# Turning the attention blocks of five batches on VectorE and through HBM instead of on TensorE, in a fused attention and feed-forward kernel

## The chip, the cores and the metric

The program runs on one core of a Trainium2 chip. The metric is the device time of one execution in microseconds (us). Engines are named as in the profile: PE is TensorE (matmuls; PEld its weight loads), DVE is VectorE, ACT is ScalarE, POOL is GpSimd, and SP is the engine that only issues DMAs (SPq its queue). SBUF is the on-chip memory, PSUM the accumulator memory that PE writes, in eight banks; HBM is the memory off the core. Each engine works through its own list of instructions strictly in order.

## The reference

Eight batches of eight heads, 576 positions of 64 channels. The output of attention is the sum of a coarse and a local part; it then goes through a two-layer network with a squared ReLU:

```python
q_d, k_d, v_d = (t.reshape(B, H, S // 4, 4, D).mean(axis=3) for t in (q, k, v))
out_up = np.repeat(sm_attn(q_d, k_d, v_d), 4, axis=2)        # coarse: 144 x 144 per head
scores = np.where(abs(i - j) < 4, scale * q @ k.T, -1e9)      # local: 7 offsets per position
x = (out_up + softmax(scores) @ v).transpose(0, 2, 1, 3).reshape(4608, 512)
y = (s * np.maximum(x @ w_in, 0) ** 2 + b) @ w_out            # 512 -> 2048 -> 512
```

All is fp32. The kernel splits the operands of the two large products into a high and a low part and makes three products of them.

## The kernel before

**The network.** The 4608 tokens are cut into 18 tiles `t` of 256, the 2048 hidden channels into 8 parts `p`. `products1(t, p)` (called G; L631) makes 24 matmuls of 256 columns into a PSUM bank `ph`, for which `split_x` must have made `xh` and `xl` of tile `t` (ACT L612, DVE L613). `upper` (called R; ACT L646 to L648: ReLU, square, cast to `gh`) and `lower` (V; DVE L653: `gl`) follow. `products2(t, p)` (H; L712 to L714) makes 12 matmuls of 512 columns into two banks `po`, in four steps of three (two row halves m, two channel halves j). After part 7 of a tile, `evict_half` (DVE L686) empties each `po` bank into `os`, and a DMA stores it; tile t+1 uses the same two banks. `ph` alternates between two banks, so that G of one (t, p) needs V of the one two before.

**The order of PE's work.** The list `order` holds the 144 pairs (t, p). The first 28 and their surroundings are laid out by a hand-written plan (`PLAN`), which this change leaves alone. From pair 28 (`BEGIN`) on a loop takes two pairs at a time and chains the matmuls by manual dependencies: 3 matmuls of G, one step of H, the rest of the first pair's G, R and V, one step of H, the second pair's G, R and V, six steps of H. At its end eight steps of H are over.

**The attention of batches 3 to 7** (the change's subject) runs beside this. Its unit of work is a *group*: four heads of one batch, in two units of two heads (`down_unit`), ten groups in all.
- *Local part* (`local_unit`), twice per group (halves `h`): `lqk` is loaded into one buffer (768 KB, L530), seven times POOL multiplies (L537, `pr`) and DVE sums (L539, `st`), a softmax of eight small DVE instructions and one ACT exp (L542 to L550), then DVE multiplies by the values (L555, L558, `pv`) and POOL or DVE adds (L559, `acc`). Positions lie on partitions here. Nine PE transposes of 128x128 (L569, `ot`) turn `acc` into the layout of `x` (channels on partitions), and six DVE additions (L573) add it to `x`.
- *Coarse part* (`down`), once per unit: DVE sums q and k by fours (L323, L325), ACT writes q into a block-diagonal operand (L330), PE makes the scores `sa` (L342), DVE and ACT the softmax `pd` (L344 to L357), six PE transposes (L365, L368, L370: `tp`, `tr`) turn it, ACT copies them to SBUF (L373, L376), PE multiplies by the values (L381, L383: `up`), and ACT spreads `up` over `x` (L519). POOL prepares the value operands (L308 to L313) into a place that the unit before's `up` must have read.

`advance` steps this work forward between the pieces of G and H, at a rate given by `need` and `free` (by which pair a batch must be ready, and from which its buffer is free); the framework then orders each engine's list by priority and a schedule of its own.

## Time and profile before

| what | us |
|---|---|
| median of 3 runs (961.5 to 962.66) | 962.63 |
| the profiled execution: its time, its span from first to last instruction | 959.7, 957.9 |
| busy in the span: PE, DVE, ACT, POOL | 924.6, 645.2, 478.2, 412.9 |
| last softmax of the attention (ACT L546) | 740.7 |
| last addition to `x` (DVE L573) | 758.1 |

The span falls into three stages: to about 250 us the plan (loading, the attention of batches 0 to 2, the first G and H); to 758 us the loop of G and H with the attention of batches 3 to 7 beside it; then G and H alone. The change touches the middle stage. In the profile's groups the engine comes behind the line (`L569 PE`), then the operation, then the tile written and the tiles read. An engine's idle time is given with what ended it.

### The profile page before, as it was taken

The page shows a single profiled execution, that of the slowest core. Times are in us where ns is not written, and L with a number is a line of the kernel's source. Part 1 is how long each engine was busy: PE and PEld are TensorE (multiplying, and loading weights), DVE is VectorE, ACT ScalarE, POOL GpSimd, SP SyncE. Part 2 cuts the span into 40 slices and gives each one's busy share as a digit, 9 for nine tenths or more (in the row PEclk, how much of TensorE's full clock was granted, in tenths as well). Part 3 has the DMA queues.
Part 4 walks back from the last instruction along what each step waited for, and adds up shares of the span by engine and source line. Part 5 has one row for each costly group of instructions (what it writes and reads, how often), then busy time and mean ns, then how long its engine had stood idle before and what let it go on. Part 6 is the DMA issues. An engine that isn't in the chain of part 4 may idle for free.

```text
span 957.9 us, 18429 instructions
## 1 busy us (share of the span) xinstructions
PE 924.6 (97%) x7316; PEld 831.1 (87%) x7316; DVE 645.2 (67%) x1134; ACT 478.2 (50%) x1133; POOL 412.9 (43%) x440
## 2 busy tenths in 40 slices
PE   6699999999999999999999999999999999999998
PEld 5588888888889989898999899889898999999997
DVE  9999999844688879787878797787877421211121
ACT  7977775466553636354544454544434333332332
POOL 6401130010587776767676768676776200000000
PEclk9699999999999999999999999999999999999999
DMA  9755413223232323323232323232311000000000
GB/s 327 264 169 179 144 47 114 71 71 102 90 107 96 110 89 108 97 91 111 83 106 81 123 79 126 80 113 91 114 54 43 1 23 1 23 1 23 1 23 22
DMA packets 32022, 86.25 MB, mean 90 GB/s; under 512 B 3520, under 2 KB 8128, under 8 KB 31936
## 3 DMA queue, kind: packets, MB, share of 16 engines
q1 hardware_dynamic: 31936, 85.08, 27.2%
q8 instruction: 57, 0.93, 0.4%
q14 instruction: 29, 0.24, 0.1%
HBM read 75.63 MB, written 9.44 MB: 89 GB/s over the span
## 4 chain that ended last, share of the span: by engine, by line
PE 54%; DVE 18%; POOL 17%; issue 5%; ACT 3%; DMA 2%; DVEq 0%; POOLq 0%; ACTq 0%
PE ph L631 24%; PE po L712 8%; POOL pr L537 8%; PE po L713 8%; PE po L714 8%; POOL acc L559 6%; DVE pv L558 3%; DVE acc L559 2%; DVE gl L653 1%; DVE st L539 1%; DVE bias L669 1%; PE sa L342 1%; DMA lqk<-in_qkn_dram 1%; PE ol L479 1%; DVE es L272 1%
## 5 line engine op out<-in xcount | busy, mean ns | idle before, releaser
L631 PE MATMUL ph<-xh,wi 128*128 128x256 f32 x2176 | 414.0, 280 | 1.6 <-DVE gl L653 1.6
L631 PEld LDWEIGHTS ph<-xh,wi 128*128 128x128 f32 x2176 | 345.2, 189 | 10.7 <-DVE gl L653 2.7
L631 PE MATMUL ph<-xl,wi 128*128 128x256 f32 x1152 | 321.6, 279 | 0.0
L537 POOL TENSOR_TENSOR pr<-lqk 128x576 f32<-128x576 f32 x140 | 206.4, 1495 | 77.0 <-DMA lqk<-in_qkn_dram 53.7
L631 PEld LDWEIGHTS ph<-xl,wi 128*128 128x128 f32 x1152 | 217.4, 189 | 7.3 <-DVE xl L771 0.2
L646 ACT ACTIVATE ph<-ph 128x512 f32<-128x512 f32 x144 | 83.9, 582 | 235.1 <-PE ph L631 227.1
L712 PE MATMUL po<-wo,gh 128*128 128x512 f32 x416 | 166.3, 400 | 4.6 <-DVE os L686 4.5
L713 PE MATMUL po<-wo,gh 128*128 128x512 f32 x416 | 164.0, 394 | 0.0
L714 PE MATMUL po<-wo,gl 128*128 128x512 f32 x416 | 162.8, 391 | 0.8 <-DVE gl L653 0.7
L653 DVE TENSOR_TENSOR gl<-ph,gh 128x512 fp32r<-128x512 f32 x104 | 71.0, 683 | 105.4 <-ACT gh L648 105.0
L539 DVE TENSOR_REDUCE st<-pr 128x9 f32<-128x576 f32 x140 | 106.2, 759 | 48.4 <-POOL pr L537 45.9
L559 POOL TENSOR_TENSOR acc<-acc,pv 128x576 f32<-128x576 f32 x80 | 115.0, 1437 | 54.0 <-DVE pv L558 31.5
L558 DVE TENSOR_TENSOR pv<-lv,st 128x576 f32<-128x576 f32 x120 | 87.3, 745 | 32.4 <-POOL acc L559 32.1
L312 POOL TENSOR_TENSOR dq<-vt 80x64 f32<-80x64 f32 x58 | 20.7, 368 | 174.5 <-PE up L383 173.3
L714 PEld LDWEIGHTS po<-wo,gl 128*128 128x128 f32 x416 | 78.1, 188 | 18.9 <-DVE gl L653 2.1
L712 PEld LDWEIGHTS po<-wo,gh 128*128 128x128 f32 x416 | 78.1, 188 | 18.6 <-DVE os L686 4.4
L713 PEld LDWEIGHTS po<-wo,gh 128*128 128x128 f32 x416 | 78.3, 188 | 11.1 <-issue 0.2
L647 ACT ACTIVATE ph<-ph 128x512 f32<-128x512 f32 x144 | 83.8, 582 | 3.7
L712 PE MATMUL po<-wo,gb 128*128 128x512 f32 x160 | 63.3, 396 | 3.5 <-DVE os L686 3.5
L648 ACT CAST gh<-ph 128x512 fp32r<-128x512 f32 x104 | 61.0, 587 | 9.5 <-PE po L713 6.7
L653 DVE TENSOR_TENSOR gb<-ph,gb 128x512 fp32r<-128x512 f32 x40 | 27.3, 682 | 53.9 <-ACT gb L648 53.9
L713 PE MATMUL po<-wo,gb 128*128 128x512 f32 x160 | 62.9, 393 | 0.0
(158 smaller groups left out, 1243.2 us busy)
## 6 DMA issues: line engine op xcount, KB each, us to landing
tqk<-in_qk_dram SPq DMA_DIRECT2D x30, 584.0 KB, 3.7
lqk<-in_qkn_dram SPq DMA_DIRECT2D x20, 768.0 KB, 4.6
lv<-in_vn_dram SPq DMA_DIRECT2D x20, 480.0 KB, 3.3
out_dram<-os SPq DMA_DIRECT2D x34, 256.0 KB, 2.3
wst<-in_moe_w_in_dram SPq DMA_DIRECT2D x7, 1024.0 KB, 5.9
wst<-in_moe_w_out_dram SPq DMA_DIRECT2D x7, 1024.0 KB, 4.9
tvd<-in_vdm_dram SPq DMA_DIRECT2D x29, 160.0 KB, 2.4
tvr<-in_vr_dram SPq DMA_DIRECT2D x29, 128.0 KB, 2.2
```

Of the source, the lines that this page charges most:

```text
L537: nc.gpsimd.tensor_tensor(pr, lqk[:, 0:CH], lqk[:, CH + o : 2 * CH + o], ALU.mult)
L539: nc.vector.tensor_reduce(ls[:, :, o], pr, AX.X, ALU.add)
L558: nc.vector.tensor_tensor(pv, lv[:, o : o + CH], w, ALU.mult)
L559: (nc.vector if o % 3 == 1 else nc.gpsimd).tensor_tensor(acc[:, :, h], acc[:, :, h], pv, ALU.add)
L631: nc.tensor.matmul(ph[:, j], wi[p][:, s, k, f], xk[:, k], start=k == 0 and s == 0 and xk is xh, stop=k == NK - 1 and s == 1)
L646: nc.scalar.activation(ph, ph, AF.Relu)
L647: nc.scalar.activation(ph, ph, AF.Square)
L648: nc.scalar.copy(gh, ph)
L653: nc.vector.tensor_tensor(gl, acc.pop((t, p)), gh.bitcast(F32), ALU.subtract)
L712: nc.tensor.matmul(po[m], gh[:, j, ms], wo[p][:, 0, j], start=first, stop=False)
L713: nc.tensor.matmul(po[m], gh[:, j, ms], wo[p][:, 1, j], start=False, stop=False)
L714: nc.tensor.matmul(po[m], gl[:, j, ms], wo[p][:, 0, j], start=False, stop=last)
```

## The change

The transposes of batches 3 to 7 leave PE. DVE turns 32x32 blocks (`nc.vector.transpose`) into a tile `ft`; a DMA writes `ft` to a tile in HBM (`far_off`, `away`), and further DMAs read it back with the blocks rearranged, so that store and loads together complete the turn.
- Local part, per group: two DVE transposes of 128x576 for nine PE transposes, one store of 576 KB, four loads of 144 KB, and two DVE additions of 128x576 (from SBUF) for six from PSUM. The additions are put off to the next group's first half, behind its softmax (`late`).
- Coarse part, per unit: two DVE transposes (96x288, 96x192) for six PE transposes and three ACT copies, two stores (108 and 72 KB), seven loads (rows of 384 or 192 bytes) back into the unit's own `pd`; ACT's write of q takes another pattern. `up` is now issued with the next unit's `sa`.
- H lags G by one step more (one step is left out in the loop's second pass; nine are over at the end). `need` of batches 3 to 7 is two pairs earlier. The qk operand is zeroed once more by POOL, and tiles change places.

The core of the diff (in `far_rest` the softmax, in `begin_far` the sums are those of `down`):

```diff
+    far_off = ctx.enter_context(
+        tc.tile_pool(name="far_off", bufs=2, space=bass.MemoryType.DRAM))
...
-    def down_unit(b, hp, banks):
+    @contextlib.contextmanager
+    def behind(engine, before=None):
...
+                tc.add_manual_dep(
+                    i, before.name,
...
+    def begin_far(b, hp):
...
+        for h in range(2):
+            hs = slice(64 * h, 64 * h + 64)
+            nc.scalar.copy(
+                qc[hs].rearrange("p i (r c) -> p i r c", c=32)[:, :, :, 16 * h : 16 * h + 16],
+                qd[hs].rearrange("p (r i c) -> p i r c", r=3, i=NQ))
+        return kd
+
+    def end_far(b, hp, both, banks):
...
+        pm = both[0:KM, 0 : 6 * GQ].rearrange("p (r n) -> p r n", r=3)
+        pr = both[:, 6 * GQ :].rearrange("p (r n) -> p r n", r=3)
+        up = banks([P, SD], "up")
+        nc.tensor.matmul(up, vdr, pr, start=True, stop=False)
+        for h in range(2):
+            nc.tensor.matmul(
+                up.rearrange("p (r n) -> p r n", r=3), vm[:, h],
+                pm[:, :, GQ * h : GQ * h + GQ], start=False, stop=h == 1)
+        return lambda: nc.scalar.copy(
             x[:, hp].rearrange("p (s j) -> p s j", j=FAC),
             up.unsqueeze(2).to_broadcast([P, SD, FAC]))
 
+    def far_chain(units, banks):
+
+        held = None
+        for b, hp in units:
+            kd = begin_far(b, hp)
+            yield
+            with tc.high_priority(), behind(nc.tensor.engine, chain_end):
+                spread = held and end_far(*held, banks)
+                scores = far_scores(kd, banks)
+            if held:
+                spread()
+            held = b, hp, (yield from far_rest(b, hp, scores))
+            yield
...
+    def far_rest(b, hp, sa):
...
+        away = {}
+        for k0, w, tag in ((0, 3, "ptm"), (KM, 2, "vt")):
+            ft = tmp([n, w, n], "ft", tag)
+            nc.vector.transpose(
+                ft.rearrange("p w (h i c) -> p w i h c", h=2, i=NQ),
+                pd[:, :, k0 : k0 + 32 * w].rearrange("p i (w h c) -> p w i h c", w=w, h=2))
+            away[k0] = far_off.tile([n, w, n], F32, name="away")
+            nc.sync.dma_start(away[k0], ft)
...
+        for w in range(3):
+            m = min(32, KM - 32 * w)
+            nc.sync.dma_start(
+                pm[32 * w : 32 * w + m],
+                away[0][:, w].rearrange("(r a) n -> a r n", r=3)[0:m])
+        for h in range(2):
+            for w in range(2):
+                at = 64 * h + 32 * w
+                nc.sync.dma_start(
+                    pr[at : at + 32],
+                    away[KM][:, w, GQ * h : GQ * h + GQ].rearrange("(r a) n -> a r n", r=3))
...
-            ot = banks([P, n, P], "ot")
-            with tc.high_priority():
-                for j in range(n):
-                    nc.tensor.transpose(
-                        ot[:, j], acc[:, i0 + j].rearrange("p h d -> p (h d)"), ident)
-            for u in range(2):
-                xv = x[:, 2 * g + u].rearrange("p (c i) -> p c i", i=CH)[:, :, i0 : i0 + n]
-                nc.vector.tensor_tensor(
-                    xv, ot[:, :, 64 * u : 64 * u + 64].rearrange("p j c -> p c j"), xv, ALU.add)
...
+        ft = two.tile([P, 4, CH * 32], F32, tag="qk", name="ft")
+        for h in range(2):
+            nc.vector.transpose(
+                ft[:, 2 * h : 2 * h + 2].rearrange("p e (i b) -> p e i b", i=CH),
+                acc[:, :, h].rearrange("p i (e a) -> p e i a", e=2))
+        away = far_off.tile([P, 4, CH * 32], F32, name="away")
+        nc.sync.dma_start(away, ft)
+        yield
+        for e in range(4):
+            nc.sync.dma_start(
+                ft[32 * e : 32 * e + 32],
+                away[:, e].rearrange("(r a) n -> a r n", r=4))
+        yield
+
+        def add():
+            with behind(nc.vector.engine):
+                for u in range(2):
+                    xv = x[:, 2 * g + u].rearrange("p (r b i) -> p r b i", r=2, b=32)
+                    nc.vector.tensor_tensor(
+                        xv, ft[:, 2 * u : 2 * u + 2].rearrange("p r (i b) -> p r b i", i=CH), xv,
+                        ALU.add)
+            complete.update((b, 2 * g + u) for u in range(2))
+
+        late.append(add)
...
+            if i % 3 == 2 and i < 30:
+                next(dn)
+            if i == NO:
+                while late:
+                    late.pop()()
+                load_pair(b, 2 * g + 1)
...
-    need = [0, 2 * HF - 3] + [(S * b // TB) * NFP - 3 for b in range(2, B)]
+    need = [0, 2 * HF - 3] + [(S * b // TB) * NFP - (3 if b == 2 else 5) for b in range(2, B)]
...
+        nc.gpsimd.memset(dq[:, 0 : 2 * GQ * NQ], 0.0)
+        dn = far_chain([(b, 2 * g + u) for b, g in GROUPS for u in range(2)], ring)
...
-            products("H", 1 * begun)
+            products("H", 1 * (st > BEGIN + 2))
...
-    products("H", 8)
+    products("H", 9)
```

How the order moves, at three places. **PE, a unit of the coarse part of batch 3.** Before, its transposes stand between two pieces of G:

```order
1118 L631 MATMUL ph<-xh,wi 128x256
1119 L365 MATMUL tp<-ident,pd 80x96
1120 L368 MATMUL tp<-ident,pd 80x96 x2
1121 L370 MATMUL tr<-ident,pd 64x96 x3
1122 L631 MATMUL ph<-xh,wi 128x256
```

Of the change (batch 4), `up` of one unit and `sa` of the next (G is L744 there, H L825 to L827):

```order
1618 L827 MATMUL po<-wo,gb 128x512
1619 L547 MATMUL up<-pd,dq 128x144
1620 L549 MATMUL up<-pd,dq 128x144 x2
1621 L577 MATMUL sa<-kd,dq 96x144 x3
1622 L744 MATMUL ph<-xh,wi 128x256
```

The transposes are gone from PE, and `up` reads `pd`, which DMAs have filled. In PE's list `up` stands two to six pairs behind the place that the unit's DVE transposes have among the V instructions.

**PE, from one tile's last H to the next tile's first** (tiles 4 and 5, numbered as `po` buffers). Before:

```order
1420 L714 MATMUL po_3755<-wo_2110,gl_4132 128x512
1421 L365 MATMUL tp_4401<-ident_115,pd_4301 80x96
1422 L368 MATMUL tp_4401<-ident_115,pd_4301 80x96 x2
1423 L370 MATMUL tr_4402<-ident_115,pd_4301 64x96 x3
1424 L631 MATMUL ph_4349<-xh_4042,wi_870 128x256
1425 L631 MATMUL ph_4349<-xl_4043,wi_870 128x256
1426 L631 MATMUL ph_4349<-xh_4042,wi_870 128x256
1427 L712 MATMUL po_4353<-wo_465,gh_4220 128x512
```

Of the change, around the old tile's last step (21 matmuls of G then stand ahead of `po_4433`, the new tile's first):

```order
1389 L744 MATMUL ph_4389<-xh_4071,wi_872 128x256
1390 L744 MATMUL ph_4389<-xl_4072,wi_872 128x256
1391 L744 MATMUL ph_4389<-xh_4071,wi_872 128x256
1392 L825 MATMUL po_3811<-wo_2112,gh_4173 128x512
1393 L826 MATMUL po_3811<-wo_2112,gh_4173 128x512
1394 L827 MATMUL po_3811<-wo_2112,gl_4174 128x512
1395 L744 MATMUL ph_4389<-xh_4071,wi_872 128x256
```

Between the old tile's last product of the first row half and the new tile's first product, which overwrites that half's bank, six matmuls of H and three of G stood, and now six of H and 24 of G.

**DVE, where the last quarter of tile 6 becomes ready** (the first that needs batch 3). Before, `xl` stands ahead of the V of pair 45, three pairs ahead of tile 6's first G, which is pair 48 (pairs are counted from 0):

```order
463 L653 TENSOR_TENSOR gb<-ph,gb 128x512
464 L539 TENSOR_REDUCE st<-pr 128x9
465 L573 TENSOR_TENSOR x<-ot,x 128x64 x2
466 L573 TENSOR_TENSOR x<-ot,x 128x64x4 x4
467 L539 TENSOR_REDUCE st<-pr 128x9 x2
468 L613 TENSOR_TENSOR xl<-x,xh 128x4x64
469 L653 TENSOR_TENSOR gl<-ph,gh 128x512
```

Of the change, the end of what stands between the V of pair 47 (row 474) and that `xl` (L686 are the late additions; rows 475 to 484 are two `st`, a `qd` and `kd`, the softmax and a `dmx`; the V of pair 48 is row 500):

```order
485 L653 TENSOR_TENSOR st<-st,lr 128x63
486 L686 TENSOR_TENSOR x<-ft,x 128x576 x2
487 L597 RECIPROCAL dsm<-dsm 96x3
488 L529 TENSOR_REDUCE qd<-tqk 128x144
489 L531 TENSOR_REDUCE kd<-tqk 128x144
490 L659 TENSOR_TENSOR acc<-lv,st 128x9x64
491 L662 TENSOR_TENSOR pv<-lv,st 128x576 x2
492 L726 TENSOR_TENSOR xl<-x,xh 128x4x64
```

The `xl` now comes behind the V of pair 47, directly ahead of pair 48. Over the whole stage, 76 V instructions stood between the first softmax of the local part and the last (19 halves), four to each; now there are 82: 4, 5, 5, 4, 2, 5 and so on, the 2 at this place.

More of the change, by code (lines that the diff above doesn't have):

```diff
@@ L500, in first_unit @@
             yield
-    def down_unit(b, hp, banks):
-        x = new_x(b)
-        tmp = lambda shape, name: one.tile(shape, F32, tag=name, name=name)
-        dn = down(b, hp, banks, tmp, diag[0])
-        next(dn)
-        next(dn)
-        add_values(b, hp, tmp, diag[0])
-        yield
-        for count in (3, 3, 2):
-            for _ in range(count):
-                next(dn)
-            yield
-        try:
-            next(dn)
-        except StopIteration as e:
-            up = e.value
-        nc.scalar.copy(
+    @contextlib.contextmanager
@@ new lines, in behind @@
+    def behind(engine, before=None):
+        traced = nc.cur_bb.bb.instructions
+        last = traced[-1]
+        before = before or next(i for i in reversed(traced) if i.engine == engine)
+        yield
+        start = next(k for k in reversed(range(len(traced))) if traced[k] is last) + 1
+        for i in traced[start:]:
+            if i.engine == engine:
+                tc.add_manual_dep(
+                    i, before.name,
+                    mybir.DependencyInfo(
+                        mybir.DependencyClass.NoSync, mybir.DependencyReason.DATA),
+                    reason="behind")
@@ new lines, in begin_far @@
+    def begin_far(b, hp):
+        qc = diag[0][1]
+        tqk = ld[(b, hp)]["qk"]
+        qt, kt = tqk[:, 0], tqk[:, 1]
+        tmp = lambda shape, name, tag: one.tile(shape, F32, tag=tag, name=name)
+        qd = tmp([P, SD], "qd", "qd")
+        kd = tmp([P, SD], "kd", "kd")
+        nc.vector.tensor_reduce(
+            qd, qt[:, 0:S].rearrange("p (s j) -> p s j", j=FAC), AX.X, ALU.add)
+        nc.vector.tensor_reduce(
+            kd, kt[:, 3 : 3 + S].rearrange("p (s j) -> p s j", j=FAC), AX.X, ALU.add)
+        for h in range(2):
[4 more added lines that the diff above has]
+        return kd
@@ new lines, in end_far @@
+    def end_far(b, hp, both, banks):
+        x = new_x(b)
+        _, _, vdr, vm = diag[0]
+        pm = both[0:KM, 0 : 6 * GQ].rearrange("p (r n) -> p r n", r=3)
[7 more added lines that the diff above has]
+        return lambda: nc.scalar.copy(
@@ L523, in local_unit @@
     def local_unit(b, g, banks):
-        acc = two.tile([P, CH, 2, D], F32, tag="qk", name="acc")
+        acc = None
         st = bank(7, [P, 2, P], "st")
@@ L551, in local_unit @@
             yield
+            acc = acc or two.tile([P, CH, 2, D], F32, tag="qk", name="acc")
             for o in range(NO):
```

58 lines of the change are left out of this document (41 added, 17 removed).

## The prediction, on record before the changed kernel ran

> **What bounds the kernel now.** The first view is the page, its busy shares:
>
> ```profile
> PE 924.6 (97%) x7316; PEld 831.1 (87%) x7316; DVE 645.2 (67%) x1134; ACT 478.2 (50%) x1133; POOL 412.9 (43%) x440
> ```
>
> PE looks like the only bound. But these are averages over three stages. The second view is busy time in a stretch, here eight tiles of the middle stage (columns: length; busy PE, PEld, DVE, ACT, POOL; clock; DMA share, GB/s):
>
> ```profile
> 335.00:737.90 402.90, 395.09 (x2666) 359.02 (x2664) 319.58 (x569) 191.83 (x491) 290.92 (x271) 1.00 0.29 93
> ```
>
> A tile takes 402.9 / 8 = 50.4 us there, and PE is idle for 1 us of it; DVE is busy for 40 and POOL for 36. In the last stage, where G and H run alone, the chain of waits shows PE's bare pace: two pairs in 774.34 - 763.38 = 10.96 us, 5.48 a pair, 43.8 a tile.
>
> ```profile
> 763.38 2.38 PE ph L631 x21
> 774.34 2.38 PE ph L631 x21
> ```
>
> The third view, the waits of the same eight tiles (us in total, times, longest), tells what DVE and POOL wait for:
>
> ```profile
> DVE st L539 <- POOL pr L537: 37.9, 43, 2.2
> POOL pr L537 <- DMA lqk<-in_qkn_dram: 35.4, 11, 6.1
> DVE pv L558 <- POOL acc L559: 28.1, 18, 3.1
> DVE gl L653 <- ACT gh L648: 3.3, 5, 1.2
> ```
>
> DVE waits 66 us for POOL, and 3.3 for the ReLU chain, which follows PE. So the attention loop of DVE and POOL hardly ever waits for PE. The fourth view says the same: followed back, the chain of waits enters this loop and, between the first and the third of these rows, holds no piece of PE.
>
> ```profile
> 469.52 1.43 POOL acc L559
> ...
> 518.99 1.43 POOL acc L559
> ...
> 535.18 0.75 DVE os L686
> ...
> 535.97 0.50 PE po L712
> ```
>
> The same place comes again after 518.99 - 469.52 = 49.5 us, one group, which the loop takes by itself; then it makes PE wait. Two bounds lie almost on each other: PE's work, and a DVE and POOL loop of 49.5 us a group. Work taken off PE is worth only what the loop lets through.
>
> **What PE loses.** Two stretches of PE's timeline price the transposes:
>
> ```profile
> 404.47 1.20 PE L569 MATMUL ot<-ident,acc 128*128 128x128 f32 x9
> 405.43 0.37 PE L631 MATMUL ph<-xh,wi 128*128 128x256 f32 x1
> 405.64 0.28 PE L631 MATMUL ph<-xl,wi 128*128 128x256 f32 x1
> ...
> 421.42 0.25 PE L365 MATMUL tp<-ident,pd 96*80 96x96 f32 x1
> 421.50 0.33 PE L368 MATMUL tp<-ident,pd 96*80 96x96 f32 x2
> 421.67 0.41 PE L370 MATMUL tr<-ident,pd 96*64 96x96 f32 x3
> 421.86 0.47 PE L712 MATMUL po<-wo,gb 128*128 128x512 f32 x1
> 422.17 0.39 PE L713 MATMUL po<-wo,gb 128*128 128x512 f32 x1
> ```
>
> The nine `ot` take 405.43 - 404.47 = 0.96, and the matmul behind them 0.21, where G's pace is 0.11: 1.06 a group. A unit's six take 421.86 - 421.42 = 0.44, and the one behind 0.31, where H's pace is 0.23: 0.52. (48 x 0.11 + 24 x 0.23 give the 10.96.) Ten groups and twenty units: 10.6 + 10.4 = **21.0 us less of PE**. `up` and `sa` keep their matmuls, in another order; the step by which H lags is only moved, from one place of PE's list to the end.
>
> **What PE's waits lose.** In the waits of the whole span the largest of PE's in this stage is
>
> ```profile
> PE po L712 <- DVE os L686: 8.0, 8, 1.9
> ```
>
> This is a new tile's first H, held until DVE has emptied the bank; DVE is late because it stands in the loop. With H one step later, 21 more matmuls of G (2.4 us) lie between, more than the longest wait of 1.9. I take **8.0 us less**; the other bound is 0, if DVE falls behind by as much again.
>
> **What the DVE and POOL loop gains.** DVE's rows for what goes, and the nearest for what comes:
>
> ```profile
> L573 DVE TENSOR_TENSOR x<-ot,x 128x256 f32<-128x256 f32 x40 | 14.1, 417 | 0.1
> L573 DVE TENSOR_TENSOR x<-ot,x 128x64 f32<-128x64 f32 x20 | 4.6, 275 | 0.2 <-PE ot L569 0.2
> L464 DVE STREAM_TRANSPOSE pt<-pl 128x384 f32<-128x384 f32 x9 | 5.1, 572 | 0.2
> L559 DVE TENSOR_TENSOR acc<-acc,pv 128x576 f32<-128x576 f32 x40 | 37.3, 932 | 3.6 <-POOL acc L559 3.6
> L558 DVE TENSOR_TENSOR pv<-lv,st 128x576 f32<-128x576 f32 x120 | 87.3, 745 | 32.4 <-POOL acc L559 32.1
> L539 DVE TENSOR_REDUCE st<-pr 128x9 f32<-128x576 f32 x140 | 106.2, 759 | 48.4 <-POOL pr L537 45.9
> L325 DVE TENSOR_REDUCE kd<-tqk 128x144 f32<-128x576 f32 x29 | 21.5, 741 | 0.0
> L545 DVE TENSOR_TENSOR st<-st,lr 128x63 f32<-128x63 f32 x20 | 4.6, 232 | 0.7
> ```
>
> Per group 4 x 0.42 + 2 x 0.27 = 2.2 us go. L464 has 1.49 ns an element of a partition; by it two transposes of 576 (0.86 each) and two units' 288 and 192 (0.43 and 0.29) come, and two additions at between 0.75 (L558) and 0.93 (L559): 4.7 to 5.0. DVE's busy time grows by some 2.6 us a group. No row has a transpose with runs as short as these (16 elements), so the upper bound is double, 5.8; a gain is excluded, since DVE does more. The middle is too far up: L464 is the same instruction and the same type, so I take 2.6. ACT loses copies and is half idle.
>
> What counts is where this lies. Take the half with the late additions, from the seventh `pr` on. DVE does `st` 0.8, seven small ones 1.6, `dmx` 0.6, a `qd` and a `kd` 1.4, the two additions 1.5, two `gl` 1.3, L555 and two `pv` 2.1, two `os` 1.5, `acc` 0.8: 11.6 before POOL may add, and POOL's next `lqk` (4.6) and two `pr` (2.8) are done by 7.4. Then come two POOL `acc` 2.9, a DVE `acc` and `pv` 1.4, two `acc` 2.9, five `pr` 7.1, the value operands 1.8: 27.7. In the other half POOL sets the pace: `lqk` 4.6, two `pr` 2.8, four `acc` 5.7, a DVE step between 1.4, five `pr` 7.1: 21.6. **Together 49.3 us a group, as now.** The far transposes and those of `acc` lie beside `pr`, where DVE waited; the additions stand in the path, but so did the `ot` ones. With the doubled transposes it is up to 52.4.
>
> PE's side: 82 pairs in 9.5 groups are 8.63 a group, at 5.48, and the two `up` and `sa`, 2.8: 50.1. So PE is the bound again, by 0.8. For halves that have too few pairs I charge **2 us** in all.
>
> **What is late next: tile 6.** Its last `xl` now stands behind the V of pair 47, and pair 48 is its first G. From the end of pair 47's G, ReLU, square, cast and `gl` take 3 x 0.58 + 0.68 = 2.4:
>
> ```profile
> L646 ACT ACTIVATE ph<-ph 128x512 f32<-128x512 f32 x144 | 83.9, 582 | 235.1 <-PE ph L631 227.1 <-DVE pv L558 5.5 <-DVE wo L277 2.4
> L653 DVE TENSOR_TENSOR gl<-ph,gh 128x512 fp32r<-128x512 f32 x104 | 71.0, 683 | 105.4 <-ACT gh L648 105.0
> ```
>
> Then DVE does two `st` 1.5, two `qd` and two `kd` 2.8, seven small ones 1.6, `dmx` 0.6, two additions 1.5, `dsm` 0.2, L555 0.75, two `pv` 1.4, `xl` 0.6: 10.9, in all 13.3. PE has six H steps (18 x 0.23 = 4.1) and one `sa` (0.65) to cover it, and stands for 8.5 us; to 11 if `dmx` waits for that `sa` and the second `qd` for its load. I take **10 us, once**. G and H are queued behind, nothing else. Every other tile has its last `xl` three pairs or more ahead.
>
> **DMAs.** The rows nearest to the round trip:
>
> ```profile
> out_dram<-os SPq DMA_DIRECT2D x34, 256.0 KB, 2.3
> tvr<-in_vr_dram SPq DMA_DIRECT2D x29, 128.0 KB, 2.2
> lqk<-in_qkn_dram SPq DMA_DIRECT2D x20, 768.0 KB, 4.6
> ```
>
> Nine issues at 0.33 of SP's time, a store's landing and a load's: 3.0 + 2.3 + 2.2 = 7.5 us. `up` stands two to six pairs (11 us or more, less the 2.4 of V) behind the transposes, so its operands are there; behind it on PE everything waits, and POOL's value operands wait for it as before. On SP, loads queue behind loads that wait for a store's landing; but each `lqk` stands where its one buffer is freed no earlier. I charge nothing; the upper bound is the third rival.
>
> **Sum.** 957.9 - 21.0 - 8.0 + 2 + 10 = 940.9 of span. The profiled execution took 959.7, 1.8 above its span, and the median of the runs is 2.9 above that: 945.6, forecast **946 us**.
>
> **Rivals.** *No wait at tile 6.* If DVE reaches those rows with PE's work still before it, 12 us fall away: 934. For it: the halves ahead have five pairs, so POOL is ahead. Against: the V of pair 47 stands in front, in DVE's own list.
>
> *DVE and POOL take the freed time.* The transposes cost double: 52.4 us a group against 50.1, and 9.5 x 2.3 = 22 in place of the 12: 956. For it: the waits above show DVE and POOL as the scarcer pair, and work goes from PE to DVE. Against: L464. The Trainium skill, "VectorE: DVE Perf Modes" (Rules for kernel authors), would turn a 128x128 on TensorE where PSUM will do as target; by that rule the change goes the wrong way, and its case is this one.
>
> *Slower, by the round trip.* PE is in order, and `up` itself waits for the seven loads. Break-even is 16.6 us over twenty units, 0.83 us of standing at each; the margin of the nearest units is about 1 to 2 us over 7.5, so it decides from a round trip of some 11 us on. At 12, about 1.5 each beyond the forecast: 976. For it: `lqk` waited up to 6.1 us for a 4.6 us load. Against: the DMA share of 0.29. The Trainium skill, "DMA: Bandwidth & Descriptors" (Specifications), wants pieces of 512 bytes for full rate, and these loads have 192 and 384; no row here shows such a load.
>
> *Nothing comes of it.* The loop's 49.5 us rule, and the pairs move with it as before: 962. Against: the order has 82 pairs there, not 76.
>
> **Chances.** Forecast 0.50, no wait 0.14, DVE and POOL 0.18, round trip 0.11, nothing 0.07. About 0.2% (1.9 us) is what a measurement of this kernel can tell from no change. Faster is the sum of the first three less a little for their edges, 0.81; within 0.2% 0.07; slower 0.12. The forecast's own range is 938 to 953; 931 to 962 takes in the first two rivals and leaves out most of the third.
>
> **What would show it.** Right: PE's idle time before a tile's first H near nothing; one PE gap of 8 to 11 us near 350 us, ended by `xl` or `sa`; 8.6 pairs in some 50 us; a DVE transpose of 576 near 0.86 us. Wrong: PE waiting at `up` for a DMA, such a transpose above 1.5 us, POOL waiting longer for `lqk` than 35 us in eight groups, or `gl` ending PE's waits throughout.

## The result

The changed kernel takes **969.1 us** (median of 7 runs, 966.7 to 973.1) against 962.3 for the kernel before in the same job (960.2 to 962.7): ratio **1.0075, 95% interval 1.0054 to 1.0097**. It is slower, where 946 was forecast. The profiled execution took 966.69, its span is 964.8.

The profile after: first the page's busy time, then eight tiles of the middle stage, from tile 5's first eviction of `os` (tiles are counted from 0) to tile 13's, in the changed kernel and in the kernel before (the prediction's eight tiles began one tile earlier, with tile 4):

```profile
PE 909.2 (94%) x7106; PEld 815.9 (85%) x7106; DVE 677.2 (70%) x1154; ACT 463.4 (48%) x1073; POOL 425.7 (44%) x441
```

```profile
393.90:791.50 397.60, 381.60 (x2506) 345.67 (x2504) 319.00 (x545) 174.67 (x425) 274.56 (x246) 1.00 0.40 121
```

```profile
385.90:782.90 397.00, 389.62 (x2626) 354.56 (x2627) 296.87 (x532) 182.97 (x455) 261.25 (x241) 1.00 0.26 84
```

PE has 120 matmuls fewer in these eight tiles, and is busy 8.0 us less. But they take 397.6 us where they took 397.0: PE is idle for 16.0 us, where it was idle for 7.4. (Before, the attention is over at 758, 25 us ahead of the end of these tiles; in the changed kernel its last addition ends at 809.7.) The last stage still runs at 10.96 us for two pairs. Ahead of these eight tiles stands the place that the prediction named, tile 6. PE's rows there (start, length, what; in brackets how long PE had stood and for whom):

```profile
366.41 0.39 PE L827 MATMUL po<-wo,gl 128*128 128x512 f32 x1
371.22 1.65 PE L577 MATMUL sa<-kd,dq 128*96 128x144 f32 x6 [4.42 <-DVE st L645]
378.10 0.58 PE L744 MATMUL ph<-xh,wi 128*128 128x256 f32 x1 [5.22 <-ACT xh L725]
381.37 0.58 PE L744 MATMUL ph<-xl,wi 128*128 128x256 f32 x1 [2.69 <-DVE xl L726]
```

PE stands 4.42 + 5.22 + 2.69 = 12.3 us, and then works at half pace, as the next view shows (columns as above; the granted clock is the number ahead of the last two):

```profile
372.00:378.00 6.00, 0.87 (x4) 0.47 (x2) 4.99 (x9) 2.05 (x10) 2.95 (x2) 0.50 0.49 187
378.00:383.00 5.00, 2.22 (x6) 1.73 (x7) 5.00 (x9) 2.42 (x7) 0.84 (x1) 0.50 0.00 0
383.00:388.00 5.00, 5.00 (x34) 4.77 (x33) 2.89 (x5) 1.29 (x3) 3.51 (x3) 0.80 0.26 63
```

PE's waits from 240 us on come to 31.1 us in all (9.8 before). The three largest, then two of DVE's and POOL's waits in the eight tiles:

```profile
PE ph L744 <- ACT xh L725: 5.2, 1, 5.2
PE ph L744 <- DVE gl L766: 4.5, 3, 2.7
PE sa L577 <- DVE st L645: 4.4, 1, 4.4
```

```profile
POOL pr L640 <- DMA lqk<-in_qkn_dram: 65.9, 12, 8.9
...
DVE qd L529 <- DMA tqk<-in_qk_dram: 14.7, 11, 3.6
```

POOL waits for `lqk` 65.9 us where it waited 35.4 (in the prediction's eight tiles), and DVE waits for `tqk`, which it hardly did before (0.7 us in the whole loop). The times of POOL's `pr` give a loop of 55.3 us a group (50.4 before). DVE's groups of instructions from 264 to 787 us give the price of the new ones:

```profile
L686 DVE TENSOR_TENSOR x<-ft,x 128x576 f32<-128x576 f32 x18 | 24.6, 1392 | 4.5 <-DMA ft<-away 4.5
L670 DVE STREAM_TRANSPOSE ft<-acc 128x576 f32<-128x576 f32 x19 | 14.8, 777 | 5.3 <-POOL acc L663 5.0
L606 DVE STREAM_TRANSPOSE ft<-pd 96x288 f32<-96x288 f32 x20 | 9.3, 465 | 0.4 <-ACT pd L599 0.4
L606 DVE STREAM_TRANSPOSE ft<-pd 96x192 f32<-96x192 f32 x20 | 6.6, 331 | 0.0
```

The chain of waits, which before went round DVE and POOL alone, now passes two loads of `tqk` and the late additions between two pieces of POOL:

```profile
415.25 1.44 POOL acc L663
...
417.96 4.43 DMA tqk<-in_qk_dram
...
423.85 3.81 DMA tqk<-in_qk_dram
...
432.01 2.34 DVE x L686
...
438.31 1.45 POOL acc L663
```

So PE's work fell and PE stood instead. A first theory was that the loop of DVE and POOL had grown longer and set the time (called theory L in the first four expectations), because `lqk` comes late and the late additions stand in DVE's path.

### The profile page after: what moved, and what is told of

The parts are those of the page before. It is cut to its first block, busy times and chain, and to the rows that moved or that the text cites. A ratio compares the mean times of both kernels' runs of the same rounds, so it can differ in the third digit from the quotient of the medians.

```text
span 964.8 us, 18482 instructions
## 1 busy us (share of the span) xinstructions
PE 909.2 (94%) x7106; PEld 815.9 (85%) x7106; DVE 677.2 (70%) x1154; ACT 463.4 (48%) x1073; POOL 425.7 (44%) x441
## 4 chain that ended last, share of the span: by engine, by line
PE 44%; POOL 20%; DVE 18%; DMA 10%; issue 4%; ACT 2%; SPq 0%; DVEq 0%; POOLq 0%; ACTq 0%
PE ph L744 20%; POOL pr L640 9%; POOL acc L663 8%; PE po L825 6%; PE po L826 6%; PE po L827 6%; DMA tqk<-in_qk_dram 5%; DMA lqk<-in_qkn_dram 3%; DVE pv L662 2%; DVE x L686 2%; DVE acc L663 2%; DVE kd L531 1%; DVE gl L766 1%; POOL vt L310 1%; DVE xl L726 1%
## 5 line engine op out<-in xcount | busy, mean ns | idle before, releaser
L744 PE MATMUL ph<-xh,wi 128*128 128x256 f32 x2176 | 412.7, 280 | 10.5 <-ACT xh L725 5.2
L744 PEld LDWEIGHTS ph<-xh,wi 128*128 128x128 f32 x2176 | 345.9, 189 | 20.6 <-ACT xh L725 5.6
L744 PE MATMUL ph<-xl,wi 128*128 128x256 f32 x1152 | 321.0, 279 | 2.7 <-DVE xl L726 2.7
L640 POOL TENSOR_TENSOR pr<-lqk 128x576 f32<-128x576 f32 x140 | 210.8, 1531 | 110.3 <-DMA lqk<-in_qkn_dram 88.0
L744 PEld LDWEIGHTS ph<-xl,wi 128*128 128x128 f32 x1152 | 218.2, 189 | 10.1 <-DVE xl L726 3.0
L825 PE MATMUL po<-wo,gh 128*128 128x512 f32 x416 | 167.0, 401 | 4.2 <-DVE dsm L597 1.9
L827 PE MATMUL po<-wo,gl 128*128 128x512 f32 x416 | 163.3, 392 | 0.7 <-DVE gl L766 0.6
L662 DVE TENSOR_TENSOR pv<-lv,st 128x576 f32<-128x576 f32 x120 | 87.3, 746 | 19.7 <-POOL acc L663 19.2
L827 PEld LDWEIGHTS po<-wo,gl 128*128 128x128 f32 x416 | 78.4, 189 | 18.7 <-DVE gl L766 1.5
L825 PEld LDWEIGHTS po<-wo,gh 128*128 128x128 f32 x416 | 78.5, 189 | 17.9 <-issue 2.9
L761 ACT CAST gh<-ph 128x512 fp32r<-128x512 f32 x104 | 61.1, 587 | 17.6 <-PE po L826 14.2
L825 PE MATMUL po<-wo,gb 128*128 128x512 f32 x160 | 63.4, 396 | 2.1 <-DVE os L799 2.1
L826 PE MATMUL po<-wo,gb 128*128 128x512 f32 x160 | 62.8, 392 | 0.0
L827 PE MATMUL po<-wo,gb 128*128 128x512 f32 x160 | 62.4, 390 | 0.0
```

The lines of the kernel that those rows point to most:

```text
L640: nc.gpsimd.tensor_tensor(pr, lqk[:, 0:CH], lqk[:, CH + o : 2 * CH + o], ALU.mult)
L662: nc.vector.tensor_tensor(pv, lv[:, o : o + CH], w, ALU.mult)
L744: nc.tensor.matmul(ph[:, j], wi[p][:, s, k, f], xk[:, k], start=k == 0 and s == 0 and xk is xh, stop=k == NK - 1 and s == 1)
L761: nc.scalar.copy(gh, ph)
L825: nc.tensor.matmul(po[m], gh[:, j, ms], wo[p][:, 0, j], start=first, stop=False)
L826: nc.tensor.matmul(po[m], gh[:, j, ms], wo[p][:, 1, j], start=False, stop=False)
```

## Experiments: which part loses

Four kernels: one order on SP, and each large part by itself. (Differences in us are of medians; where two kernels ran in different jobs, their ratios to before give the same within about 1 us.)

**`lqk` ahead of the second `tqk`.**

```diff
-            lqk = one.tile(...); nc.sync.dma_start(lqk, ...)      # at the half's start
+            lqk = ahead.pop() if h else load_lqk(b, g, 0)
...
+                if h == 0 and o == NO - 1:
+                    with tc.high_priority():
+                        ahead.append(load_lqk(b, g, 1))
```

> The changed kernel, but the second half's lqk load of a group is issued on SP ahead of the load of the group's second tqk, not behind it. Theory L (the DVE and POOL loop became the bound: 55.3 us a group by the marks of POOL's pr and acc, against 50.4 before; 3.1 of the 4.9 are POOL's longer wait for lqk in the second half, the rest late additions of 1.39 us in DVE's path to the weights): the wait before that half's first pr falls from 7.8 us towards 5, the loop to 52.5 to 54, the time to 957 to 965. Rival S (one stall at tile 6 and the clock behind it are the loss, 16 us, and the rest is as foreseen): 969, no change. Rival D (the small pieces of the round trips slow every load): lqk still lands late, at most 2 us gained: 967 to 969.

974.3 us, ratio to before 1.0137 (1.0121 to 1.0153): 5 us *slower* than the changed kernel. But the order asked for did not come about. In this run's trace SP still issues `lqk` behind the second `tqk` of a group (at 426.90 behind 426.45, at 483.06 behind 482.62), and POOL waits 6.7 us on average ahead of the second half's first `pr`, as in the changed kernel (not the 7.8 of the expectation). There `lqk` goes out at 424.30, and POOL has read its one buffer only at 423.65 (the `pr` from 416.64 on), so no order on SP could have sent it much earlier. The run says nothing on theory L, and why it is slower is not known.

**The later H alone**, in the kernel before.

```diff
-            products("H", 1 * begun)
+            products("H", 1 * (st > BEGIN + 2))
...
-    products("H", 8)
+    products("H", 9)
```

> The kernel before with one part of the change alone: w_out's products one unit later (H a step behind). The prediction's step 3 says that PE's waits for os, 8.0 us, go: 954. Theory L: PE no longer waits there, but the loop of 50.4 us a group is unchanged and the wait turns up elsewhere on PE: 957 to 962.

953.4 us, 0.9921 (0.9907 to 0.9935): 7.7 us gained, where the prediction's step 3 had 8.0. PE's waits for `os` are 0.9 us in all.

**Only the coarse part by VectorE and HBM** (the local part by `ot`, as before, but added late).

```diff
-        ft = two.tile([P, 4, CH * 32], F32, tag="qk", name="ft")
-        ... transposes, store, four loads ...
         def add():
-            with behind(nc.vector.engine): ... tensor_tensor(xv, ft[...], xv, ALU.add)
+            for i0 in range(0, CH, 4): ... nc.tensor.transpose(ot[:, j], acc[...], ident) ...
```

> The changed kernel, but the local part is turned by TensorE as before (nine ot a group, six additions from PSUM), at the late place that the additions now have; only the coarse part goes through VectorE and HBM. PE has 10.6 us more than in the changed kernel. Theory L: the two late additions of 2.8 us a group become 2.2, the local trip's store and four loads leave SP, so the loop falls by 1 to 2 us a group and gives back about what PE takes: 962 to 970. Rival S: the late completion of tile 6 stays, and PE's 10.6 come on top: 972 to 980. Rival D: 180 of the 220 small loads and stores stay, time 970 to 980.

**943.9 us**, 0.9818 (0.9801 to 0.9835), faster than every expectation: 9.5 us better than the later H alone, of the 10.4 that `tp` and `tr` cost PE. Its page and, of PE's waits from 240 us on, the largest and the one for the coarse round trip:

```profile
PE 910.4 (97%) x7196; PEld 819.6 (87%) x7196; DVE 654.5 (70%) x1174; ACT 463.6 (49%) x1073; POOL 413.6 (44%) x441
```

```profile
PE ot L674 <- POOL acc L663: 2.2, 3, 1.2
...
PE up L547 <- DMA pd<-away: 0.8, 1, 0.8
```

PE waits 0.8 us for the coarse round trip in the whole run, and there is no stall at tile 6, though `need` has the same due times and the local addition the same late place in the code. One thing more differs from the changed kernel: these additions are not tied behind another of DVE's instructions (`behind` in the diff). What that tie costs comes further down.

**Only the local part by VectorE and HBM** (`down_unit` of before, with `tp`, `tr` and its own `up`).

```diff
-        dn = far_chain([...], ring)
+        dn = chain(*(down_unit(b, 2 * g + u, banks) for u in range(2)))
```

> The changed kernel, but the coarse part is turned by TensorE as before (tp and tr, up as soon as its operands are there); only the local part goes through VectorE and HBM, with late additions. PE has 10.4 us more than in the changed kernel; the fourteen small loads a group and the four DVE transposes are gone. Theory L: the late additions in the path stay and lqk is less late with an emptier SP, the loop 53 to 55 us a group: 965 to 975. Rival D: without the small pieces tqk and lqk land as before, the loop is 51: 958 to 964. Rival S: tile 6's stall stays, and PE's 10.4 come on top: 975 to 980.

976.1 us, 1.0152 (1.0131 to 1.0173): 22.7 us slower than the later H alone. The four kernels agree: the coarse part gains 9.5 us without the local part and 7.0 beside it (976.1 to 969.1), most of what it takes off PE, and the local part's way, with its tied additions, **loses 25.2 us** (969.1 against 943.9), though it takes 10.6 off PE.

## Experiments: what of the local part's way

**Three tiles on the qk buffers, not four.** In the changed kernel `acc`, `ft` and two `tqk` share two buffers. SP's issues (start, length):

```profile
417.52 0.34 SPq L674 DMA_DIRECT2D away<-ft  x1
417.96 0.38 SPq L156 DMA_DIRECT2D tqk<-in_qk_dram  x1
420.68 2.03 SPq L677 DMA_DIRECT2D ft<-away  x4
423.85 0.35 SPq L156 DMA_DIRECT2D tqk<-in_qk_dram  x1
424.30 0.38 SPq L633 DMA_DIRECT2D lqk<-in_qkn_dram  x1
```

The two `tqk` of a group and `lqk` are loaded within 7 us, the first once `acc` has been turned, where before the two were 14 us apart. The edit turns `acc` by way of two `pv` buffers and loads back into `acc`'s own tile:

```diff
-        ft = two.tile([P, 4, CH * 32], F32, tag="qk", name="ft")
+            half = two.tile([P, 2, CH * 32], F32, tag="pv", name="half")
+            nc.vector.transpose(half..., acc[:, :, h]...)
+            nc.sync.dma_start(away[:, 2 * h : 2 * h + 2], half)
+        ft = acc.rearrange("p i h d -> p (i h d)").rearrange("p (e n) -> p e n", e=4)
```

> The changed kernel with the same transposes, round trip and late additions, but without the fourth tile on the two qk buffers: acc is turned into two pv buffers, one store of 288 KB from each, and the four loads come back into acc's own tile. So the buffers turn over as before: two tqk and acc, not two tqk, acc and ft. Theory B (the changed kernel loses by this: tqk's two loads of a group stand in series behind acc's last addition, 418.0 and 423.9 us, next to lqk at 424.3, while with the local part on TensorE they were issued 14 to 24 us apart and ahead of need): tqk's loads spread again, the loop falls from 55.3 to 52 to 53 us a group, the stall at tile 6 goes, and with 10.6 us less on PE than with the local part on TensorE (943.9) the time is 933 to 942. Rival A (the two late additions of 1.39 us in DVE's path are the loss): 965 to 969. Rival D (the round trip itself, its five issues on SP and its bytes): 967 to 971, one issue more.

954.6 us, 0.9934 (0.9916 to 0.9951): 14.5 us gained, about half of what theory B claims. PE still waits 5.4 us for `xh` at tile 6. DVE's wait for `tqk` from 264 to 800 us did not fall (21.2 us, against 18.6 in the changed kernel), so by which wait the fourth tile costs its 14.5 us is not shown.

**Late additions left out.**

```diff
-                    nc.vector.tensor_tensor(xv, ft[...], xv, ALU.add)
```

> The changed kernel with the late additions left out (the local part is not added to x; all transposes, stores and loads stay). Rival A: the 2.8 us a group in DVE's path were the loss, time 943 to 950, tile 6's stall at most 6 us. Theory B: the path is shorter by 2.8 us a group, but tqk and lqk come as late: 955 to 963. Rival D: 960 to 969.

948.1 us, 0.986 (0.9836 to 0.9884): 21.0 us gained, rival A's number. Whether for rival A's reason is asked of the next runs.

**Without the store and the loads.**

```diff
-        nc.sync.dma_start(away, ft)
-            nc.sync.dma_start(ft[32 * e : 32 * e + 32], away[:, e]...)
```

> The changed kernel with the local part's round trip left out: ft is turned by VectorE and added as it stands (so the local part lands in the wrong rows), without the store and the four loads of a group; the fourth tile on the qk buffers, the late additions and the coarse part's round trips stay. Rival D: without the five DMAs a group SP is free for lqk, and the time is 943 to 955. Theory B: tqk still waits until acc is turned, only some 0.4 us a group earlier: 962 to 969. Rival A: 965 to 969.

965.7 us, 1.0052 (1.0032 to 1.0073): 3.4 us, with an interval that overlaps the changed kernel's. Neither the bytes nor SP's five issues are the loss.

**Straight reads in the late additions** (on the kernel with three tiles).

```diff
-                half.rearrange("p e (i b) -> p e i b", i=CH),
+                half.rearrange("p e (b i) -> p e i b", i=CH),
```

> As the kernel that brings the local part back into acc's tile, but the transposes write with a stride of nine elements, so that the late additions read straight runs instead of elements 32 apart. If the addition's 1.39 us come from that reading, it takes 0.75 as pv does, the path falls by 1.3 us a group and the time by 0 to 6 us against that kernel. If they come from something else, 1.39 and no change. The transposes lie beside POOL's pr and cost nothing up to 1.5 us each.

954.8 us, no change. DVE's two groups:

```profile
L671 DVE STREAM_TRANSPOSE half<-acc 128x576 f32<-128x576 f32 x19 | 24.3, 1281 | 0.2 <-POOL acc L663 0.2
L687 DVE TENSOR_TENSOR x<-acc,x 128x576 f32<-128x576 f32 x18 | 15.4, 881 | 1.6 <-DMA acc<-away 1.6
```

The addition falls from 1364 ns to 881 on average (1222 to 757 in the median, as a few take some 2 us), the transposes rise from 766 to 1281: the price of the scattered order moves to whoever pays it.

**Both cures: three tiles, no late additions** (the diffs of those two).

> The changed kernel with both edits: the local part comes back into acc's tile (three tiles on the qk buffers), and the late additions are left out (the local part is not added to x). Alone they took 14.5 and 21.0 us off the changed kernel's 969. If these two are all that the local part's way through HBM costs, what is left is the kernel with only the coarse part turned so (943.9) less the 10.6 us of its ot on PE and the 2.2 us a group of its additions: 930 to 937. If both shorten the same stretch of the loop (acc, transposes, tqk, weights), the gains overlap: 942 to 948.

946.4 us, 0.9833 (0.982 to 0.9845). The gains overlap, and what is left is no better than the kernel that keeps `ot` on PE (943.9). So even with the loss gone, PE's 10.6 us buy nothing.

**The local transposes left out** (the store takes `acc` itself).

```diff
-            nc.vector.transpose(ft[:, 2 * h : 2 * h + 2]..., acc[:, :, h]...)
-        nc.sync.dma_start(away, ft)
+        nc.sync.dma_start(away, acc...)
```

> The changed kernel with the local part's two DVE transposes (0.78 us each) left out: acc goes to HBM as it stands, so the local part lands in the wrong rows; store, loads, late additions and the fourth tile stay. The prediction's step: they lie beside POOL's pr and cost nothing: 966 to 969. Theory W (DVE and POOL pace each other so closely that any us of DVE's costs about 0.75, as the late additions did, 21 us for 28): 1.56 us in ten groups by 0.75, 955 to 960.

980.8 us, 1.0185 (1.0166 to 1.0203): 11.7 us *slower* with less work. Now the store reads `acc`, so the buffer is free only when it has landed. SP's rows of one group:

```profile
420.14 0.34 SPq L670 DMA_DIRECT2D away<-acc  x1
...
424.78 0.43 SPq L156 DMA_DIRECT2D tqk<-in_qk_dram  x1
```

`tqk` goes out 4.6 us behind the store, not 0.4. The edit had this side effect and does not price the transposes. `x` is complete later than in any other kernel (the first table of the next section).

**DVE's time alone, in two places.** On the kernel without late additions, four reductions a group whose result nobody uses, 40 of 740 ns:

```diff
+        def extra(src):
+            with behind(nc.vector.engine):
+                for _ in range(4):
+                    nc.vector.tensor_reduce(one.tile([P, CH], ...), src[:, 0:CH], AX.X, ALU.add)
...
+                if h == 0 and o == 3: extra(lqk)     # beside pr
...
+            if h == 0: extra(lv)                     # the other kernel: behind the weights in the code
```

> The changed kernel without the late additions (948.1), with four reductions a group of what POOL reads (as st, 0.76 us each, 3.0 us a group, result not used) put among the st of the first half, where DVE waited for POOL's pr. The prediction's step, that work beside pr is free: 948 to 953. Theory W: 948 + 0.75 x 30, 966 to 972.

957.9 us (0.9948, 0.9929 to 0.9968): 9.7 for 29.6 us of DVE, between the two expectations.

> The same four reductions, of lv, but between the first half's weights and its first pv, where the late additions stood. Both theories: the loss of the late additions comes back, 965 to 972. If it stays at 948 to 953, it was not DVE's time there that the late additions cost, but what they wait for (their loads from HBM and the tile that they hold).

**949.9 us** (0.9872, 0.9854 to 0.989): 1.7 us. But the reductions do not stand where the late additions stood. DVE's rows of one group (L659 is the weights' last instruction):

```profile
369.72 0.71 DVE L632 TENSOR_REDUCE extra<-lv 128x9 f32<-128x576 f32 x1
...
373.65 0.74 DVE L632 TENSOR_REDUCE extra<-lv 128x9 f32<-128x576 f32 x1
...
385.99 0.23 DVE L659 TENSOR_TENSOR st<-st,lr 128x63 f32<-128x63 f32 x1
```

Of the 40, 12 come like these ahead of the weights, beside `pr`, 22 between the products, and only 6 between the weights and the first product, where 18 of the 20 late additions are. So the run does not price that place. It shows that 29.6 us of DVE's time, spread over the first half, can cost next to nothing. And it shows that a longer loop does not set the time by itself: from POOL's first `pr` of group 2 to that of group 10 the loop takes 56.1 us a group here ((746.4 - 297.8) / 8) and 55.3 in the changed kernel ((735.4 - 292.9) / 8), which is 19.2 us slower. That speaks against rival A, and against the first theory. What the unused reductions do not do is hold a tile, wait for loads, and finish `x`.

## Experiments: the lag

Next theory, called L again in the expectations, for lag: PE stands because `x` is complete late. The rows of the changed kernel at batch 3's end, POOL's last addition to `acc` and then DVE's:

```profile
361.92 1.43 POOL L663 TENSOR_TENSOR acc<-acc,pv 128x576 f32<-128x576 f32 x1
```

```profile
363.39 0.78 DVE L670 STREAM_TRANSPOSE ft<-acc 128x576 f32<-128x576 f32 x1
...
374.33 3.27 DVE L686 TENSOR_TENSOR x<-ft,x 128x576 f32<-128x576 f32 x2
...
380.90 1.54 DVE L726 TENSOR_TENSOR xl<-x,xh 128x256 fp32r<-128x256 f32 x2
```

From the end of `acc` (363.35) to a complete `x` (377.6) are 14.2 us, and tile 6's `xl` ends at 382.4; PE had stood since 366.8, but for one `sa`. With `ot` on TensorE:

```profile
351.43 2.93 POOL L663 TENSOR_TENSOR acc<-acc,pv 128x576 f32<-128x576 f32 x2 [1.54 <-DVE acc L663]
```

```profile
358.27 1.40 DVE L678 TENSOR_TENSOR x<-ot,x 128x256 f32<-128x256 f32 x4
...
361.52 0.42 DVE L678 TENSOR_TENSOR x<-ot,x 128x64 f32<-128x64 f32 x2
...
365.19 1.22 DVE L719 TENSOR_TENSOR xl<-x,xh 128x1024 fp32r<-128x1024 f32 x1
```

There it is 354.36 to 361.9, 7.6 us (the 4.6 of the next expectation leaves out the last additions), and `xl` ends at 366.4, 16 us earlier. The late additions are tied behind the instruction that DVE last got (`behind(nc.vector.engine)`), which puts them behind the next half's weights, where 374.33 is.

**The lag taken away, all work kept.** Base: the kernel without store and loads (965.7).

```diff
-            with behind(nc.vector.engine):
```

> As the kernel whose local part stays in its ft (no store, no loads, wrong rows; 965.7), with one thing changed: the two late additions are no longer tied behind DVE's last instruction at that place, so they move from behind the next half's weights to behind the transposes. DVE's work is the same to the instruction. Theory L (lag: from acc's last addition to a complete x are 14 us in the changed kernel, 363.4 to 377.6 for batch 3, and 4.6 with the local part on TensorE, 354.4 to 359.0; PE has no other work and stands): the lag falls to about 5 us, the stall at tile 6 goes, 943 to 953. Rival W (the additions cost by DVE's time in the loop, wherever they stand): 960 to 967.

952.1 us (0.9903, 0.9885 to 0.9921): **13.6 us** by moving the additions alone. DVE's rows of the same place:

```profile
360.96 0.78 DVE L670 STREAM_TRANSPOSE ft<-acc 128x576 f32<-128x576 f32 x1
...
363.02 2.96 DVE L680 TENSOR_TENSOR x<-ft,x 128x576 f32<-128x576 f32 x1
...
368.87 1.22 DVE L720 TENSOR_TENSOR xl<-x,xh 128x1024 fp32r<-128x1024 f32 x1
```

The lag is 5.1 us, and PE's wait for `xh` falls from 7.6 us to 3.2, though the additions are longer (1.47 us in the median against 1.23, the second one here 2.96). The rival is out. But moving them changed a second thing: the additions also read `ft` earlier, so its buffer comes free earlier, and DVE's wait for `tqk` from 264 to 800 us falls from 20.0 us to 2.8. This run does not part the lag from the buffers.

**The same tie off in the whole changed kernel.** The diff is that one line again.

> The changed kernel, whole, with only that tie taken off the late additions. They need their loads from HBM, so they can move only from behind the weights to between them, some 1 us earlier. Theory L: the lag of 14 us stays, as it is the trip's, and so does the time: 965 to 969. If the place alone made the loss, 945 to 955.

958.0 us (0.9968, 0.9954 to 0.9982): 11.1 us better than the change as made, and faster than the kernel before. The expectation missed: the lag is 10.9 us and not 14, as the additions stand ahead of the weights, and wait 14.2 us in all for their loads. DVE's wait for `tqk` falls here too, from 18.6 us to 8.6.

**`ot` put back on PE beside the new way**, its result unused.

> The changed kernel with the nine ot transposes on PE put back beside the new way, their result unused: 10.6 us more of PE's work, in front of the local transposes. If PE set the time, 979 to 981. By theory L PE stands 31.5 us there for DVE and takes it in while it would stand: 967 to 973. That is what the local part's way off PE would have been worth at best.

973.5 us (1.0124, 1.01 to 1.0147), at the upper edge of the second expectation: 10.6 us of PE's work cost 4.4, so PE took most of it in while it would have stood.

**Three tiles and the tie off** (the diffs of those two).

> The whole change with both cures: the local part comes back into acc's own tile (alone 954.6), and the late additions are not tied behind DVE's last instruction (alone 958.0). Everything is computed. If lag and tile turnover are two parts of one loss, and together all of it, the time comes to that of the kernel with neither additions nor fourth tile, 946, within 3 us: 943 to 950. If something else of the local part's way costs as much, 951 to 956.

960.4 us (0.9994, 0.9979 to 1.0008), worse than either cure and above both expectations. Of DVE's waits from 264 to 800 us:

```profile
DVE x L687 <- DMA acc<-away: 25.9, 9, 5.4
```

The additions now stand ahead of their loads, and everything on DVE behind them. This kernel's `xl` of tile 6 is done at 371.9, and PE waits 8.2 us for `os` instead. It looks as if the trip's latency were paid at DVE here and at PE in the changed kernel; no run shows that by itself.

**The best version**: only the coarse part, the later H, and the due times of before.

```diff
-    need = [...] + [(S * b // TB) * NFP - (3 if b == 2 else 5) for b in range(2, B)]
+    need = [...] + [(S * b // TB) * NFP - 3 for b in range(2, B)]
```

> The kernel with only the coarse part turned by VectorE and HBM (943.9), with the table of due times as before the change: each batch due two pairs later (3 ahead of its tile, not 5). If it is the early due time that keeps the late additions from a stall, tile 6 stands some 5 us: 947 to 951. If the batch has slack, the work is spread more evenly: 941 to 944.

**940.8 us, 0.9789 (0.9773 to 0.9804)**: 2.1% faster than before. So it is not the earlier due time that keeps this kernel from a stall; the batch has slack. PE is busy 97% of the span, so little is left in this order of work.

The end of tile 6's `xl` and the time go together in the kernels that have no attention transposes of these batches on PE and add the local part to `x` (us):

| kernel | lag, batch 3 | `xl` of tile 6 ends | time |
|---|---|---|---|
| stays, additions early | 5.1 | 370.1 | 952.1 |
| three tiles, tie off | 11.2 | 371.9 | 960.4 |
| three tiles | 14.1 | 373.7 | 954.6 |
| three tiles, straight reads | 13.4 | 375.6 | 954.8 |
| tie off | 10.9 | 376.4 | 958.0 |
| stays | 15.2 | 380.4 | 965.7 |
| **the change** | 14.2 | 382.4 | 969.1 |
| `lqk` first | 16.0 | 385.2 | 974.3 |
| no local transposes | 19.6 | 385.9 | 980.8 |

One row stands out of order, the one in which DVE waits for its loads. The lag alone orders them less well: with three tiles `acc` itself is ready earlier.

Tile 6 is not all of it. The same marks as in the result, tile 5's and tile 13's first eviction of `os`, cut the profiled executions in three (us; one execution each, the one with the tie off was the fastest of its nine):

| kernel | to tile 5's eviction | eight tiles | to the end |
|---|---|---|---|
| before | 385.9 | 397.0 | 175.0 |
| only the coarse part | 379.0 | 387.2 | 175.1 |
| **the change** | 393.9 | 397.6 | 173.3 |
| tie off | 389.2 | 388.3 | 173.9 |

Against the kernel with only the coarse part the change loses 14.9 us up to the end of the stall at tile 6 and 10.4 in the eight tiles behind it. Taking the tie off gives back 4.7 and 9.3.

## Why the prediction was wrong

- **The two bounds close together**: right, and more so than was drawn. PE's freed time found no taker beyond the coarse part: taking `ot` off as well leaves 946.4 at best, and that without the late additions.
- **PE loses 21.0 us**: the work went, though PE's busy time fell by 15.4 only. For the coarse half the time followed, 9.5 of 10.4. The local half was not to be had.
- **PE's waits for `os`, 8.0 us**: right alone, 7.7 measured; in the changed kernel 3.1 of the 8.0 are still there.
- **The DVE and POOL loop stays at 49.3**: wrong, 55.3. The transposes were sized well (0.47, 0.33 and 0.78 us against 0.43, 0.29 and 0.86). The late additions take 1.39 us on average (1.22 in the median), not 0.75: they read elements 32 apart, and the row taken (L558) reads straight runs. But neither this size nor the loop's length decided by itself: a kernel with a loop of 56.1 us takes 949.9. What the step left out is that `ft` is a fourth tile on the two qk buffers, so that `tqk` waits for `acc` and lands beside `lqk`; three tiles gave 14.5 us back. That work beside `pr` is free was wrong too: 29.6 us of it cost 9.7.
- **Tile 6, 10 us once, and 2 us in all for every other wait: the steps that failed, the second by more.** The span is 964.8 - 940.9 = 23.9 us above the sum. Term by term: PE's busy time is 5.6 us above the forecast (15.4 for 21.0; most likely the half pace behind the stalls); its waits for `os` are 3.1 and not 0; tile 6's stall, ended by `sa`, `xh` and `xl` as foreseen, is 12.3 and not 10; and all PE's other waits, 1.8 before and 2 more in the sum, are 31.1 - 12.3 - 3.1 = 15.7, 11.9 too many. The 1.0 that is left is idle time in no wait. PE waits for `xh` and `xl` at tile 6 alone, as the prediction said; the other waits are for `gl`, `dq`, `dsm`, `up` and the like, in tiles where PE was thought to be the bound. The first step counted DVE's instructions from PE's side and never asked how long after `acc` the `x` is whole: 14.2 us. The second rested on the loop of 49.3 us with PE as the bound, and on additions that hold nothing up. The runs show in their place what the local part's way costs: without it 943.9 us and 6.5 us of PE's waits; with it, but the tie off, 11.1 us less than the change. Which of the later waits come of the lag and which of the buffers stays open.
- **DMAs charged nothing**: right for the coarse trip (PE waits 2.8 us at `up` in all) and for the bytes (3.4 us without the local trip), but `tqk` and `lqk` land later than it assumed; what that costs is not shown.
- **The rivals**: the sign was that of the slower one, and a round trip is part of it, the local one; but the rival put the price at `up`, where PE waits 2.8 us in all. "DVE and POOL take the freed time" holds for the local half, though not by doubled transposes. The Trainium skill, "VectorE: DVE Perf Modes" (Rules for kernel authors), cited there, prefers TensorE for a 128x128: the local part comes out that way (25.2 us lost, though not by the transposes' own 0.78 us), the 96x144 of the coarse part the other way (9.5 us gained). The Trainium skill, "DMA: Bandwidth & Descriptors" (Specifications), wants pieces of 512 bytes for full rate. What smaller ones cost is not shown here: the loads of 18 KB, four in five of them in pieces of 192 bytes, land in 1.8 us (the page's list of DMA issues after):

```profile
pd<-away SPq DMA_DIRECT2D x100, 18.0 KB, 1.8
```

Open is how the loss of 22.7 us (969.1 to 946.4) divides between the lag and the turnover of the buffers: alone they give 11.1 and 14.5, together 8.7, most likely because then DVE waits. Not run: the kernel with `ot` on PE and its additions tied, which would price the tie without the trip. Why unused reductions cost 9.7 us in one arrangement and 1.7 in the other was not followed up.

## What to carry over

Taking work off the busiest engine pays only as far as the result is still there in time: count from the last producer to the moment the consumer may start, through store, loads, issue slots and the place in an in-order queue, and compare it with the work that the consumer still has. A tile that must outlive a round trip also holds a buffer: here, to bring the result back into a tile that was there already was worth 14.5 us. Do such a change part by part: here one half was worth 7 to 9.5 us and the other cost 23 to 25. And read an edit's effect from the order that the trace shows: two of the edits here (`lqk` first, and the reductions behind the weights) left the instructions elsewhere than meant.

## Unexpected of the hardware

PE's clock does not come back with its work. The changed kernel's PE at tile 6, and the windows behind:

```profile
381.96 0.63 PE L825 MATMUL po<-wo,gh 128*128 128x512 f32 x1
382.39 0.63 PE L826 MATMUL po<-wo,gh 128*128 128x512 f32 x1
```

```profile
384.00:385.00 1.00, 1.00 (x7) 1.00 (x6) 0.52 (x1) 0.00 (x0) 1.00 (x1) 0.52 0.38 113
385.00:386.00 1.00, 1.00 (x11) 1.00 (x11) 0.73 (x1) 0.00 (x0) 1.00 (x3) 1.00 0.14 33
```

At the end of its stand of 4.42 us the granted clock fell to 0.50, some 4.5 us after the last matmul (366.8 to about 371.3), and stayed so until about 385.0, 3.6 us after steady work began at 381.37; H's matmuls stood 0.43 us apart instead of 0.23, about 1.8 us lost on top of the 12.3. The Trainium skill, "TensorE: Matmul & The Clock Gate" (What's actually happening), gives about 3.4 us for both turns. The way up agrees. The way down can be quicker: in the kernel that stays with early additions PE's last matmul ahead of tile 6 starts at 362.90, PE stands 3.18 us, and the clock has begun to fall ahead of 366 (the number ahead of the last two):

```profile
362.90 0.39 PE L821 MATMUL po<-wo,gl 128*128 128x512 f32 x1
```

```profile
365.00:366.00 1.00, 0.00 (x0) 0.00 (x0) 1.00 (x2) 0.00 (x0) 0.05 (x1) 0.86 0.00 0
```

An addition of 576 elements that reads one operand at a distance of 32 elements takes 1.22 us in the median against 0.76 in straight runs, and a DVE transpose that writes nine elements apart 1.28 us against 0.77.
